# Projecting half of the queries with tokens on partitions, in plain float32, in a linear-attention and gated-MLP kernel

## The chip, the cores and the metric

The kernel runs on one core of a Trainium2 chip. The metric is the device time of one execution in microseconds (us), less is better. The engines named below are the profile's: PE is TensorE's matmul stream, PEld its weight loads, DVE is VectorE, ACT is ScalarE, POOL is GpSimd, and SP is SyncE, whose queue (SPq) issues every DMA of this kernel.

## The reference

Attention with a feature map, followed by a gated feed-forward layer with a convolution over tokens:

```python
# q, k, v: (8 batches, 8 heads, 576 tokens, 64); w_phi: (64, 128)
def phi(x):
    proj = np.einsum('bhsd,df->bhsf', x, w_phi)
    proj = proj - np.max(np.abs(proj), axis=-1, keepdims=True)
    return np.concatenate([np.exp(proj), np.exp(-proj)], axis=-1)
q_p, k_p = (phi(q), phi(k))
kv = np.einsum('bhsf,bhsd->bhfd', k_p, v)
z = np.sum(k_p, axis=2)
num = np.einsum('bhsf,bhfd->bhsd', q_p, kv)
den = np.einsum('bhsf,bhf->bhs', q_p, z)[..., None] + 1e-06
attn = num / den                       # heads joined: x is (8, 576, 512)

h = np.maximum(x @ w_in, 0.0)          # w_in (512, 1024)
conv_out = sum(conv_w[k] * h shifted by k - 1 tokens, for k in 0..2)
out = (h / (1 + np.exp(-conv_out))) @ w_out   # w_out (1024, 512)
```

## The kernel before, in words

**Tiling.** The 8 heads of a batch are taken as two units of four heads, numbered `qd` 0 and 1, so that there are 16 units. A unit holds two stacks, and a stack holds a pair of heads, 64 features of each, on the 128 partitions. Its tokens are cut into five groups: group 0 is one tile of 128 tokens (the last 64 tokens of both stacks), groups 1 to 4 are two tiles each (`n` is 1 or 2). So a unit has nine tiles of 128 tokens by two heads.

**Precision.** Where a number has to be kept to float32, most of the kernel splits it into a float32r high part and a float32r remainder and multiplies three times (high by high, high by low, low by high). In a few places it multiplies plain float32 numbers, which shows in the trace as two MATMUL records for one instruction.

**Queries.** A group of queries must end as feature-major values in PSUM (features on partitions, tokens along the row), less the largest absolute value of each token's projection, on which ACT takes two exponentials (L399). The kernel has two ways to get there.

- *Tokens on partitions* (the `lo is None` branch, batches 0 and 1, which is what `NQ_F32 = 4` units means). One DMA loads the group (L191). `project` multiplies each tile once by the float32 weights of both heads (L220); DVE takes the absolute maximum (L228) and subtracts it (L230) into an SBUF tile called `qs`; PE transposes the result, two transposes for a tile, against an identity (L353). The projection and the transposed values each take one PSUM tile of the ring `gq`, which has two.
- *Features on partitions* (batches 2 to 7). Two DMAs load the group twice, once to each half of the partitions (L196). ACT writes the float32r rounding of it (L199), and POOL replaces the lower half by the remainder (L200). Two matmuls with stationary weights write the whole group, 512 columns wide for two tiles (L360, L364). DVE takes the maximum over blocks of 32 features with a transpose (L368), ACT moves three of four blocks together (L371, three small instructions), DVE finishes the maximum (L375 to L379), one small DMA writes it into two rows of the operand (L380), and a third matmul subtracts it in PSUM (L386). One PSUM tile of `gq` holds the group throughout.

After that both ways are the same: exponentials, a split into high and low parts (L60, L65), and the products with `kv` (`nm`, L420 and L432), between whose matmuls the next unit's key products (`kv`, L275 and L279) are placed one by one. Then ACT moves numerators and denominators out (L454, L459), and `x_process` divides.

**The feed-forward part.** Half a batch of tokens (288) is one step: `h_part` is 96 matmuls (`hp`, L509), `conv_process` does convolution and gate on POOL, DVE and ACT, `o_part` is 96 matmuls (`op`, L572) whose results ACT moves out (L577) ahead of a DMA.

**What sets the order.** The program is emitted by a planner at the end of the function. Attention groups are generators in a window of 16, the feed-forward part is one more generator, and each yields estimated PE times (`pe(330 * n)` for a projection, `pe(220 * n)` for its transposes; `pe(230 * n)` and `pe(115 * n)` for the other way) and waits. The planner compares how much of `ATT_PE` and `MOE_PE` is left and steps one or the other. Steps of attention from batch 1 on are given a priority offset of 300 for the scheduler, which orders each engine's instructions; some are given high priority beside it (the features-on-partitions maximum, the third matmul, the exponentials). Each engine works its own queue in order.

The functions that the difference touches, with the profile's line numbers:

Of the kernel before, what the change touches and what calls it, by code (L numbers as in the profile page):

```python
# [15 lines left out]
B, H, S, D = 8, 8, 576, 64  # L16
# [3 lines left out]
NQ = 2  # L20
# [10 lines left out]
NQ_F32 = 4  # L31
# [4 lines left out]
def kernel(  # L36
# [20 lines left out]
    def split(src, hi, lo, eng_hi, eng_lo):  # L57

        if eng_hi is nc.scalar:
            nc.scalar.activation(out=hi, in_=src, func=AF.Copy)  # L60
        elif eng_hi is nc.gpsimd:
            nc.gpsimd.tensor_scalar(out=hi, in0=src, scalar1=1.0, scalar2=0.0, op0=ALU.mult, op1=ALU.add)  # L62
        else:
            nc.vector.tensor_copy(out=hi, in_=src)
        eng_lo.tensor_tensor(out=lo, in0=src, in1=hi.bitcast(F32), op=ALU.subtract)  # L65
# [118 lines left out]
    def group_columns(g):  # L184
        return (512, 1) if g == 0 else ((g - 1) * 256 + (P if g > 2 else 0), 2)

    def load_split(src, b, qd, g, kind):
        c0, n = group_columns(g)
        if kind == "q" and 2 * b + qd < NQ_F32:
            raw = sb.tile([P, n * P], F32, name=f"{kind}r{b}_{qd}_{g}", tag=kind + "r", bufs=2)  # L190
            nc.sync.dma_start(out=raw, in_=src[b, qd, :, c0 : c0 + n * P])  # L191
            return n, raw, None
        if kind == "q":
            raw = sb.tile([P, 2, n * P], F32, name=f"qr{b}_{qd}_{g}", tag="qr", bufs=2)
            for h in range(2):
                nc.sync.dma_start(out=raw[D * h : D * h + D, :, :],  # L196
                                  in_=src[b, qd, :, c0 : c0 + n * P].rearrange("(i d) s -> d i s", d=D))
            x = sb.tile([P, 2, n * P], F32R, name=f"qx{b}_{qd}_{g}", tag="qs", bufs=2)
            nc.scalar.activation(out=x, in_=raw, func=AF.Copy)  # L199
            nc.gpsimd.tensor_tensor(out=x[D:P], in0=raw[D:P], in1=x[D:P].bitcast(F32), op=ALU.subtract)  # L200
            return n, x, x
        raw = sb.tile([P, n * P], F32, name=f"{kind}r{b}_{qd}_{g}", tag=kind + "r", bufs=2)
        nc.sync.dma_start(out=raw, in_=src[b, qd, :, c0 : c0 + n * P])
        hi = sb.tile([P, n * P], F32R, name=f"{kind}xh{b}_{qd}_{g}", tag=kind + "xh", bufs=2)
        lo = sb.tile([P, n * P], F32R, name=f"{kind}xl{b}_{qd}_{g}", tag=kind + "xl", bufs=2)
        split(raw, hi, lo, nc.gpsimd, nc.gpsimd)
        return n, hi, lo
# [36 lines left out]
    def k_process(b, qd, g):  # L244
# [4 lines left out]

        yield until(back("kp", 2), back("kv", 4))  # L250
        n, hi, lo = load_split(kT, b, qd, g, "k")
        v0 = 16 if g == 0 else 4 * (g - 1)
        v = sb.tile([P, 4 * VW], F32, name=f"v{b}_{qd}_{g}", tag="v", bufs=3)
# [77 lines left out]
    def q_process(b, qd, g):  # L331
# [4 lines left out]

        yield until(back("qp", 2))
        n, hi, lo = load_split(qT, b, qd, g, "q")
        yield wait(3000)
        yield until(back("tp", 2))  # L340
# [266 lines left out]
        active.append([now[0], g, False, lead[0]])  # L607

    MOE_PE = 2 * B * (8 * 1480 + 4 * 2960)
    ATT_PE = B * (18 * 330 + 72 * 215 + 18 * 345 + 8 * 6 * 270 + 4 * 250) + NQ_F32 // NQ * 18 * 205  # L610
    TAIL = TAIL_US * 1000
    left = {"a": ATT_PE, "m": MOE_PE}
    start = {}
# [28 lines left out]
    while moe is not None or chains or active:  # L642
        while chains and sum(1 for p in active if p[2]) < WINDOW:
            b, x, g, kind = chains.pop(0)
# [82 lines left out]
```

## Time and profile before

| | |
|---|---|
| median of 3 runs | 827.03 us (826.72 to 830.36) |
| profiled execution, time | 827.25 us |
| profiled execution, span from first to last instruction | 825.5 us |
| PE busy / PEld busy | 775.8 us / 744.0 us |
| DVE / ACT / POOL busy | 649.4 us / 627.4 us / 316.1 us |
| instructions | 17295 |
| mean granted TensorE clock | 0.981 |
| moved by DMA | 56.44 MB |

Durations below come from the one profiled execution. A MATMUL's recorded duration holds its latency, and neighbours overlap; what one costs in a dense stream is the distance from its start to the start of the next. Every busy time is that of the engine alone, so the engines' times overlap.

### The profile page before, as it was taken

To read this page: it belongs to the slowest core of one execution; us is meant where nothing else is said; L and a number is where in the kernel's file an instruction comes from. 1 tells how busy PE (TensorE), PEld (TensorE's weight loads), DVE (VectorE), ACT (ScalarE), POOL (GpSimd) and SP (SyncE) were. 2 spreads that over 40 slices of the span, in tenths; PEclk is the share of its full clock that TensorE was granted. 3 is DMA by queue.
4 is the path that set the end of the run, shared out by engine and by line. 5 is a ranking of instruction groups with operands and counts; after the bars stand their busy time and mean duration, and the time that the engine had idled before them with its cause. 6 is when DMAs were issued, how large, how long until landed. Compare 5 with 4: busy or idle time off the path is not lost. (4 is left out here: it accounts for less than half of the span.)

```text
span 825.5 us, 17295 instructions
## 1 busy us (share of the span) xinstructions
PE 775.8 (94%) x5972; PEld 744.0 (90%) x5972; DVE 649.4 (79%) x1378; ACT 627.4 (76%) x1372; POOL 316.1 (38%) x395
## 2 busy tenths in 40 slices
PE   6988889899999999999999999999999899999997
PEld 5866789798989889999989999999999899999997
DVE  5898999796887968889788798788888587766451
ACT  4787886859898797988888888798988779744322
POOL 5765564262524424344243352525335232211120
PEclk9998989989999999999999999999999899999999
DMA  5544422212222122222222222222222111000001
GB/s 168 179 131 122 130 65 70 66 37 68 67 64 74 38 84 68 68 71 66 78 68 65 69 70 63 70 61 74 62 81 59 51 39 31 10 30 30 22 23 43
DMA packets 66814, 56.44 MB, mean 68 GB/s; under 512 B 17832, under 2 KB 64680, under 8 KB 66728
## 3 DMA queue, kind: packets, MB, share of 16 engines
q1 hardware_dynamic: 66728, 55.35, 23.3%
q8 instruction: 47, 0.77, 0.4%
q14 instruction: 39, 0.32, 0.1%
HBM read 45.21 MB, written 9.44 MB: 66 GB/s over the span
## 5 line engine op out<-in xcount | busy, mean ns | idle before, releaser
L279 PEld LDWEIGHTS kv<-v,ke 128*128 128x128 f32 x1024 | 156.5, 195 | 10.8 <-ACT ke L260 5.2
L279 PE MATMUL kv<-v,ke 128*128 128x65 f32 x1024 | 161.4, 256 | 4.3 <-ACT ke L260 4.2
L539 DVE SCALAR_TENSOR_TENSOR c<-h,cw,c 128x288 f32<-128x288 f32 (+1 forms) x256 | 144.7, 574 | 23.1 <-POOL c L534 21.1
L534 POOL TENSOR_SCALAR c<-h,cw 128x288 f32<-128x288 f32 x128 | 82.3, 645 | 207.2 <-ACT h L517 142.7
L572 PE MATMUL op<-gh,wout_hi 128*128 128x288 f32 x512 | 153.0, 299 | 5.9 <-ACT os L577 5.0
L509 PE MATMUL hp<-xh,win_hi 128*128 128x290 f32 x512 | 154.2, 302 | 4.2 <-ACT h L517 3.3
L572 PE MATMUL op<-gl,wout_hi 128*128 128x288 f32 x512 | 152.3, 298 | 0.9 <-DVE gl L65 0.9
L509 PE MATMUL hp<-xl,win_hi 128*128 128x290 f32 x512 | 153.1, 299 | 0.1
L509 PE MATMUL hp<-xh,win_lo 128*128 128x290 f32 x512 | 152.7, 298 | 0.0
L572 PE MATMUL op<-gh,wout_lo 128*128 128x288 f32 x512 | 152.0, 297 | 0.0
L200 POOL TENSOR_TENSOR qx<-qr,qx 64x512 fp32r<-64x512 f32 (+1 forms) x60 | 77.6, 1294 | 111.2 <-ACT qx L199 102.3
L65 DVE TENSOR_TENSOR ql<-qe,qh 128x512 fp32r<-128x512 f32 x112 | 90.0, 822 | 22.0 <-ACT qh L60 21.7
L509 PEld LDWEIGHTS hp<-xh,win_hi 128*128 128x128 f32 x512 | 97.6, 191 | 7.5 <-ACT h L517 5.4
L572 PEld LDWEIGHTS op<-gh,wout_hi 128*128 128x128 f32 x512 | 97.0, 190 | 7.5 <-ACT os L577 5.9
L572 PEld LDWEIGHTS op<-gl,wout_hi 128*128 128x128 f32 x512 | 97.1, 190 | 1.7 <-DVE gl L65 1.2
L509 PEld LDWEIGHTS hp<-xl,win_hi 128*128 128x128 f32 x512 | 97.9, 191 | 0.7 <-DVE xl L65 0.2
L509 PEld LDWEIGHTS hp<-xh,win_lo 128*128 128x128 f32 x512 | 97.7, 191 | 0.5
L572 PEld LDWEIGHTS op<-gh,wout_lo 128*128 128x128 f32 x512 | 97.2, 190 | 0.5
L62 POOL TENSOR_SCALAR kxh<-kr 128x256 fp32r<-128x256 f32 (+1 forms) x80 | 42.3, 529 | 130.8 <-issue 62.6
L517 ACT ACTIVATE h<-hp 128x290 f32<-128x290 f32 x128 | 50.8, 405 | 40.1 <-PE hp L509 39.6
L432 PE MATMUL nm<-ql,kvh 128*65 128x256 f32 x224 | 69.5, 310 | 0.2 <-DVE ql L65 0.2
L432 PE MATMUL nm<-qh,kvl 128*65 128x256 f32 x224 | 69.2, 309 | 0.0
(99 smaller groups left out, 1879.3 us busy)
## 6 DMA issues: line engine op xcount, KB each, us to landing
qr<-in_qT_dram SPq DMA_DIRECT2D x112, 128.0 KB
v<-in_vt_dram SPq DMA_DIRECT2D x80, 130.0 KB
out_dram<-os SPq DMA_DIRECT2D x64, 144.0 KB
kr<-in_kT_dram SPq DMA_DIRECT2D x64, 128.0 KB
w_r<-in_w_in_dram SPq DMA_DIRECT2D x8, 512.0 KB
w_r<-in_w_out_dram SPq DMA_DIRECT2D x8, 512.0 KB
rr<-rc SPq DMA_DIRECT2D x128, 2.2 KB
qr<-in_qT_dram SPq DMA_DIRECT2D x28, 64.0 KB
```

The costliest lines, as they stand in the source:

```text
L62: nc.gpsimd.tensor_scalar(out=hi, in0=src, scalar1=1.0, scalar2=0.0, op0=ALU.mult, op1=ALU.add)
L65: eng_lo.tensor_tensor(out=lo, in0=src, in1=hi.bitcast(F32), op=ALU.subtract)
L200: nc.gpsimd.tensor_tensor(out=x[D:P], in0=raw[D:P], in1=x[D:P].bitcast(F32), op=ALU.subtract)
L279: ins = nc.tensor.matmul(out=kp[i][:, s, p0 : p0 + VW], lhsT=lhsT, rhs=v[:, (2 * t + i) * VW : (2 * t + i + 1) * VW], start=False, stop=(g ...
L432: ins = after(ins, lambda: nc.tensor.matmul(out=ps[:, i, o : o + w], lhsT=w_, rhs=x_, start=(k == 0), stop=(k == 5)))
L509: nc.tensor.matmul(out=ps, lhsT=w_, rhs=x_, start=(k == 0), stop=(k == 11))
L517: nc.scalar.activation(out=h4[:, f % 4, :], in_=ps, func=AF.Relu)
L534: nc.gpsimd.tensor_scalar(out=cv, in0=hs[:, o : o + TC], scalar1=cw[:, f, 1:2], scalar2=0.0, op0=ALU.mult, op1=ALU.add)
L539: nc.vector.scalar_tensor_tensor(out=cv[:, lo:hi], in0=hs[:, o + j - 1 + lo : o + j - 1 + hi], scalar=cw[:, f, j : j + 1], in1=cv[:, lo:hi ...
L572: nc.tensor.matmul(out=ps, lhsT=w_, rhs=x_, start=(k == 0), stop=(k == 23))
```

## The change

From batch 2 on, the units with `qd == 0` (the first half of each batch's queries) are loaded, projected and transposed as in batches 0 and 1; the units with `qd == 1` stay with features on partitions. Six of the twelve later units move, that is, six groups of one tile and 24 groups of two. Exponentials, splits, products and everything behind them stay. The planner's total for attention gets half of the difference between the two ways for each moved batch.

```diff
+    def plain(b, qd):
+
+        return 2 * b + qd < NQ_F32 or qd == 0
+
     def load_split(src, b, qd, g, kind):
         c0, n = group_columns(g)
-        if kind == "q" and 2 * b + qd < NQ_F32:
+        if kind == "q" and plain(b, qd):
             raw = sb.tile([P, n * P], F32, name=f"{kind}r{b}_{qd}_{g}", tag=kind + "r", bufs=2)
             nc.sync.dma_start(out=raw, in_=src[b, qd, :, c0 : c0 + n * P])
             return n, raw, None
...
     MOE_PE = 2 * B * (8 * 1480 + 4 * 2960)
-    ATT_PE = B * (18 * 330 + 72 * 215 + 18 * 345 + 8 * 6 * 270 + 4 * 250) + NQ_F32 // NQ * 18 * 205
+    ATT_PE = B * (18 * 330 + 72 * 215 + 18 * 345 + 8 * 6 * 270 + 4 * 250) + (NQ_F32 // NQ + (B - NQ_F32 // NQ) / 2) * 18 * 205
```

## The prediction

> **What bounds the kernel now.** I read the page first (busy times and the slices of the clock), then the busy time by stretch, then the chain that ended last, then PE's waits inside the middle stretch, and at last PE's instructions in order of time, to price the two ways of projecting.
>
> ```profile
> PE 775.8 (94%) x5972; PEld 744.0 (90%) x5972; DVE 649.4 (79%) x1378; ACT 627.4 (76%) x1372; POOL 316.1 (38%) x395
> PEclk9998989989999999999999999999999899999999
> ```
>
> PE is the fullest engine, but a share over the whole span mixes stages. By stretch (start to end, length, then busy us with the number of instructions for PE, PEld, DVE, ACT and POOL, then the granted clock and DMA):
>
> ```profile
> 60.00:100.00 40.00, 34.06 (x218) 28.65 (x216) 35.88 (x72) 31.62 (x68) 23.46 (x23) 0.91 0.46 131
> 100.00:140.00 40.00, 36.21 (x269) 34.01 (x270) 39.87 (x76) 30.52 (x69) 21.17 (x24) 0.91 0.23 63
> 165.00:717.00 552.00, 531.19 (x4220) 515.78 (x4221) 451.99 (x1017) 463.95 (x1048) 212.60 (x259) 0.99 0.22 62
> 717.00:825.50 108.50, 103.88 (x771) 102.87 (x769) 55.12 (x94) 39.18 (x64) 13.80 (x25) 1.00 0.08 28
> ```
>
> From 165 to 717 us, where batches 2 to 7 run, PE is busy 531.19 of 552 us, so only 20.8 us are there to be won back, while ACT has 88 us free and DVE 100. From 717 us only feed-forward matmuls are left, and the chain that ended last is one row of them after another:
>
> ```profile
> 717.28 12.80 PE op L572 x96
> 730.08 13.11 PE hp L509 x96
> ```
>
> So PE's own work is the bound in both stretches: a microsecond of work added to PE is a microsecond at the end, unless it fills one of the 20.8 idle ones. PE's waits in the middle stretch are these (us, times, longest):
>
> ```profile
> PE op L572 <- ACT os L577: 5.0, 3, 4.2
> PE qp L386 <- DMA qx<-qmp: 3.4, 4, 1.4
> PE hp L509 <- ACT h L517: 3.3, 6, 1.5
> PE kp L223 <- ACT num L459: 3.1, 2, 2.6
> PE qp L360 <- POOL qx L200: 2.8, 3, 1.1
> PE kv L279 <- ACT ke L260: 2.1, 2, 1.6
> PE qp L360 <- ACT qe L399: 1.1, 1, 1.1
> ```
>
> The chain of a features-on-partitions query group accounts for 3.4 + 2.8 + 1.1 = 7.3 us of them; the other ACT rows for 5.0 + 3.3 + 3.1 + 2.1 = 13.5 us.
>
> **The change part by part: PE's work.** Both ways are in this trace, and both stand somewhere in a dense stream, so I take start-to-start distances. A group of two tiles in plain float32 (batch 1), and one with features on partitions (its three matmuls, here of neighbouring groups), and two matmuls of a one-tile group:
>
> ```profile
> 134.85 1.03 PE L220 MATMUL qp<-wbd_f,qr 128*128 128x256 f32 x4
> 135.71 0.60 PE L353 MATMUL tp<-idn,qs 128*128 128x128 f32 x4
> 136.15 0.28 PE L420 MATMUL nm<-qh,kvf 128*65 128x64 f32 x2
> ...
> 334.28 0.39 PE L360 MATMUL qp<-qx,wq_hi 128*128 128x512 f32 x1
> 334.51 0.40 PE L386 MATMUL qp<-qx,wq_m 128*128 128x512 f32 x1
> 334.75 0.40 PE L364 MATMUL qp<-qx,wq_lo 128*128 128x512 f32 x1
> 334.99 0.28 PE L223 MATMUL kp<-wbd_hi,kxh 128*128 128x256 f32 x1
> ...
> 341.13 0.28 PE L360 MATMUL qp<-qx,wq_hi 128*128 128x256 f32 x1
> 341.25 0.28 PE L364 MATMUL qp<-qx,wq_lo 128*128 128x256 f32 x1
> 341.37 0.30 PE L572 MATMUL op<-gh,wout_lo 128*128 128x288 f32 x1
> ```
>
> Plain: 135.71 - 134.85 = 0.86 us for the projection (four records for two instructions) and 136.15 - 135.71 = 0.44 us for four transposes, 1.30 us together; a one-tile group is half, 0.65. Features on partitions: 334.99 - 334.28 = 0.71 us; a one-tile group is 3 x 0.12 = 0.36. A unit has four groups of two and one of one, so it costs 4 x 1.30 + 0.65 = 5.85 us against 4 x 0.71 + 0.36 = 3.20 us. The six moved units add 6 x 2.65 = **15.9 us** to PE. The weight loads of both ways hide beside matmuls in these distances already.
>
> The Trainium skill's page "TensorE: Matmul & The Clock Gate", section "Back-to-back issue gap", gives columns / 2.4 + 2.5 ns for the gap between matmuls when warm, which is 56 ns for a transpose's 128 columns. By that, an estimate, four transposes would take 0.22 us, the six units 6 x 4.5 x 0.22 = 5.9 us less, and PE's extra work would be 10.0 us. The trace differs (0.44 us), and I go by the trace.
>
> **What the other engines lose and gain.** Over all 60 features-on-partitions groups, the instructions on the tile `qx` (columns PE, PEld, ACT, POOL) and on `qmt` (DVE, ACT) were busy:
>
> ```profile
> 0.00:825.50 825.50, 56.10 (x180) 30.53 (x180) 35.49 (x60) 77.62 (x60) 0.98 0.24 68
> ```
>
> ```profile
> 0.00:825.50 825.50, 62.34 (x180) 38.24 (x180) 0.98 0.24 68
> ```
>
> Half of the groups go. ACT loses (35.49 + 38.24) / 2 = 36.9 us and gains nothing. POOL loses 38.8 us. DVE loses 31 us of maximum work there, and gains the plain maximum and subtraction:
>
> ```profile
> L230 DVE TENSOR_TENSOR qs<-qp,qm 128x512 f32<-128x512 f32 x16 | 10.8, 678 | 0.0
> L228 DVE TENSOR_REDUCE qm<-qp 128x4 f32<-128x512 f32 x16 | 10.8, 678 | 0.4 <-PE qp L220 0.4
> ```
>
> 24 x 1.36 + 6 x 0.68 = 36.6 us. (Two small DVE instructions a group, L377 and L379, also go, so DVE comes out about level.) None of this is on the path by itself: DVE, ACT and POOL have slack in the middle stretch. If that cover went, 36.6 us of DVE work would be the price; level DVE work is why I cost it at nothing.
>
> What relief on ACT is worth must be bounded. At one end nothing; at the other all 13.5 us of PE's waits on ACT. ACT goes from 84% (463.95 of 552) to about 77% of the stretch, and 4.2 of the 13.5 us are a single wait, so I take a quarter, **-3.4 us**. Of the chain's own 7.3 us of waits I take the moved half, **-3.65 us**; the ends are 0 and -7.3.
>
> **What SP's queue loses.** For each moved group one load in place of two and no small DMA:
>
> ```profile
> L196 SPq DMA_DIRECT2D qr<-in_qT_dram x120: 598/645/1379, 135.9 to 680.4; - x120
> L380 SPq DMA_DIRECT2D qx<-qmp x60: 642/678/738, 155.3 to 702.2; - x60
> ```
>
> That is 0.645 + 0.678 = 1.3 us of issue a group, some 40 us over 30 groups. A load's buffer now comes free when PE has projected the group two back, and no longer when POOL has subtracted:
>
> ```profile
> SPq L196 <- POOL qx L200: 46.4, 35, 4.3
> SPq L191 <- PE qp L220: 2.3, 3, 1.4
> ```
>
> A load that waits holds back the key, value, denominator, reciprocal and output DMAs behind it. These rows say 1.3 us a wait before (46.4 / 35) and 0.8 after (2.3 / 3), so I count no new loss here, and no gain, since the PE waits above name loads nowhere; the ends are 0 and the 3.4 us of PE's waits on DMA, counted already.
>
> **New waits.** The plain way takes two PSUM tiles of `gq` where the other takes one, and PE waits for DVE between projection and transposes. While batch 1 went this way (90 to 160 us, ten groups), PE waited for:
>
> ```profile
> PE qp L220 <- ACT qe L399: 1.2, 1, 1.2
> PE tp L353 <- DVE qs L230: 1.0, 1, 1.0
> PE qp L220 <- PE kv L279: 0.4, 1, 0.4
> ```
>
> 2.6 us for ten groups, so 7.8 us for 30 at that rate; the other end is 0. In that stage DVE was busy 39.87 of 40 us (from 100 us) against 452 of 552 in the stretch where the moved units will run, so I take half, **+3.9 us**. Behind a waiting transpose stands every later matmul, feed-forward ones too, since PE works in order.
>
> **The sum.** 827.25 (the profiled execution; 1.75 us of it lie outside its span) + 15.9 - 3.65 - 3.4 + 3.9 = **840.0 us**. The execution stands 0.2 us above the median of the runs, which I leave in the rounding.
>
> **The rivals.**
>
> *Relief wins* (faster). PE's waits on ACT are the place. If all 13.5 us go, with the chain's 3.65, and with them the stretch at half clock that followed the 4.2 us wait,
>
> ```profile
> 642.00:648.80 6.80, 5.38 (x21) 5.28 (x22) 1.29 (x2) 3.67 (x10) 1.12 (x1) 0.50 0.20 63
> ```
>
> worth half of 6.8, the time is 827.25 + 15.9 - 13.5 - 3.65 - 3.4 = 822.6 us. It decides from the point where the relief passes 15.9 us; the difference can be measured from about 20.0. For it: ACT is the releaser in most PE waits. Against: all of PE's idle time there is 20.8 us, and ACT keeps 93% of its work in the stretch. Chance 0.06.
>
> *Relief just pays* (the same rows, about three quarters of them): 828 us, chance 0.09.
>
> *The ring and DVE bite*. The full 7.8 us of new waits, one more stretch at half clock after one of them (3.4 us), no relief: 827.25 + 15.9 + 7.8 + 3.4 = 854 us. For it: the rows of batch 1 above. Against: the density of DVE there. Chance 0.10.
>
> *The plain way cools PE*. In the two stretches of 40 us from 60 to 140 us, where units of the plain way run, the granted clock is 0.91; that is 2 x 40 x 0.09 = 7.2 us lost in about two units. At 3.6 us a unit, six moved units lose 21.6 us: 840 + 21.6 = 862 us. Against: PE was idle 5.9 of 40 us from 60 us on and 3.8 from 100, which can explain it without the transposes, and 0.44 us of transposes in the some 9 us that a group has (552 / 60) is little. Chance 0.03. The same page of the Trainium skill, section "Part 4: PE-mode transpose", says that a transpose does not count as PE being busy for the clock gate; by that rule this rival is the outcome. The trace cannot separate it from idle time, since both stand in the same stretches.
>
> **How the numbers follow.** The forecast case has 0.72 and gives 840 us; its own range is 831 to 850. Relief wins 0.06, relief just pays 0.09, the ring 0.10, cooling 0.03. Changes under 0.5% (4.1 us) can't be told from none here. Faster 0.06; same 0.09; slower 0.72 + 0.10 + 0.03 = 0.85. The range, 829 to 852 us, leaves out relief that wins, part of the even case, cooling and most of the ring: about 0.18.
>
> **What the changed profile would show.** L220 and L353 at 72 + 6 x 9 x 2 = 180 records each; L360, L364, L386 and the ACT and POOL work on `qx` at half; ACT some 37 us less busy, POOL 39 less, DVE within a few us. PE's distances for a moved group at 0.86 + 0.44 us. The last stretch unchanged at about 108 us, starting 12 or 13 us later. PE's waits on `qx` and `qmp` about halved, and a few us of waits at L220 and L353. Wrong it would be if PE's idle time from 165 us on fell well below 10 us, if the stretch showed several pieces at half clock, or if the scheduler's new order moved waits of other matmuls (L509, L572, L279) by more than the 3.4 us that I gave them.

## The result and the profile after

The changed kernel takes 838.42 us (median of 7 runs, 832.95 to 842.06) against 827.03 us before (7 runs, 825.63 to 830.36): a ratio of 1.012, 95% interval 1.0089 to 1.0151, so 11.4 us slower. The forecast was 840.0 us. The execution that was profiled took 832.95 us, the fastest of the seven, which has to be kept in mind below: its span is 5.6 us longer than that of before, half of what the medians say.

Page and busy time by stretch of the changed kernel (columns: start and end, length, busy us with the number of instructions for PE, PEld, DVE, ACT and POOL, granted clock, DMA share, GB/s); the last two stretches meet where its last rows of feed-forward matmuls begin (723 us):

```profile
PE 784.6 (94%) x6098; PEld 755.0 (91%) x6098; DVE 633.9 (76%) x1288; ACT 598.0 (72%) x1252; POOL 266.1 (32%) x365
PEclk9998999999999999999999999999999999999999
```

```profile
165.00:717.00 552.00, 535.33 (x4289) 521.89 (x4288) 428.94 (x913) 429.06 (x918) 162.65 (x227) 0.99 0.20 56
165.00:723.00 558.00, 541.33 (x4334) 527.89 (x4333) 433.12 (x922) 432.44 (x926) 164.37 (x230) 0.99 0.20 56
723.00:831.10 108.10, 103.96 (x771) 102.96 (x769) 55.24 (x94) 39.27 (x65) 13.88 (x25) 1.00 0.08 28
```

The chain that ended last:

```profile
723.36 12.80 PE op L576 x96
736.16 13.12 PE hp L513 x96
```

The last stretch is as long as before (108.1 against 108.5 us) and starts 6 us later, where the prediction had 12 or 13. Over the whole span ACT fell by 29.4 us and POOL by 50.0. Between 165 us and there PE is idle 16.7 us in place of 20.8, and yet that stretch is longer, because PE has more to do. PE's waits in it (from L187 on, lines are 4 higher than before):

```profile
PE kp L227 <- ACT num L463: 4.0, 3, 1.6
PE qp L224 <- ACT qe L403: 2.2, 1, 2.2
PE hp L513 <- ACT os L581: 2.2, 2, 1.5
PE op L576 <- ACT os L581: 1.5, 2, 1.1
PE qp L364 <- issue: 1.2, 1, 1.2
PE hp L513 <- ACT h L521: 1.0, 1, 1.0
PE nm L436 <- DVE ks L234: 1.0, 1, 1.0
PE qp L390 <- DMA qx<-qmp: 0.9, 1, 0.9
PE qp L364 <- POOL kxh L62: 0.7, 1, 0.7
```

The projection and transposes stand where the change put them (six units more, 72 records to 180):

```profile
L224 PE MATMUL qp<-wbd_f,qr 128*128 128x256 f32 x180 | 51.3, 397 | 11.0 <-ACT qh L403 4.3 <-DMA qr<-in_qT_dram 3.2 <-ACT qe L403 2.8
L357 PE MATMUL tp<-idn,qs 128*128 128x128 f32 x180 | 33.9, 274 | 1.8 <-DVE qs L234 1.5 <-ACT qh L403 0.2
```

Part of both spans ran at half clock. Inside the stretch from 165 us these are the pieces of before (two, of which 642.00:648.80 stands in the prediction) and of after:

```profile
164.10:170.90 6.80, 4.99 (x21) 4.98 (x22) 6.80 (x11) 6.36 (x15) 2.83 (x3) 0.50 0.13 38
```

```profile
164.70:168.10 3.40, 3.40 (x17) 3.39 (x16) 3.40 (x7) 1.93 (x5) 1.09 (x3) 0.50 0.26 77
707.40:710.80 3.40, 3.14 (x13) 3.13 (x14) 1.96 (x3) 3.31 (x8) 0.51 (x1) 0.50 0.14 46
```

In such a piece a matmul of the feed-forward part starts 0.241 us after the one ahead of it, here in before:

```profile
643.83 0.44 PE L572 MATMUL op<-gl,wout_hi 128*128 128x288 f32 x1
644.07 0.44 PE L572 MATMUL op<-gh,wout_lo 128*128 128x288 f32 x1
```

At full clock the distance is 0.134 us. So 1 - 0.134 / 0.241 = 0.44 of PE's busy time in these pieces is lost: from 165 us on 0.44 x (4.99 + 5.38) = 4.6 us before, and 0.44 x (3.10 + 3.14) = 2.8 us in the profiled execution after (the first 0.3 us of its first piece lie ahead of 165 us). PE's work at full clock grew by (541.33 - 2.8) - (531.19 - 4.6) = 11.9 us, idle time fell by 4.1 and lost clock by 1.8, which leaves the 6 us. This is not yet all of the added work: ten records of L224 that the change added stand ahead of 165 us. The table at the end of the experiments takes the whole span.

### The profile page after: what moved, and what is told of

It reads as the page before. It is cut to its first block, busy times and chain, and to the rows that moved or that the text cites. A ratio compares the mean times of both kernels' runs of the same rounds, so it can differ in the third digit from the quotient of the medians.

```text
span 831.1 us, 17133 instructions
## 1 busy us (share of the span) xinstructions
PE 784.6 (94%) x6098; PEld 755.0 (91%) x6098; DVE 633.9 (76%) x1288; ACT 598.0 (72%) x1252; POOL 266.1 (32%) x365
## 4 chain that ended last, share of the span: by engine, by line
PE 61%; DVE 15%; ACT 13%; DMA 5%; issue 4%; SPq 1%; POOL 1%; ACTq 0%; DVEq 0%; POOLq 0%
PE hp L513 18%; PE op L576 17%; PE kv L283 7%; PE nm L436 7%; DVE c L543 4%; PE qp L224 3%; DMA den<-dr 2%; PE kp L227 1%; ACT c L547 1%; PE tp L357 1%; ACT dr L458 1%; ACT num L463 1%; DVE xf L489 1%; DMA rr<-rc 1%; PE kp L228 1%
## 5 line engine op out<-in xcount | busy, mean ns | idle before, releaser
L543 DVE SCALAR_TENSOR_TENSOR c<-h,cw,c 128x287 f32<-128x287 f32 (+1 forms) x256 | 144.2, 573 | 31.7 <-POOL c L538 29.9
L283 PEld LDWEIGHTS kv<-v,ke 128*128 128x128 f32 x1024 | 154.3, 193 | 9.2 <-ACT ke L264 3.9
L538 POOL TENSOR_SCALAR c<-h,cw 128x288 f32<-128x288 f32 x128 | 78.2, 613 | 261.7 <-ACT h L521 171.2
L283 PE MATMUL kv<-v,ke 128*128 128x65 f32 x1024 | 159.6, 254 | 2.2 <-ACT ke L264 1.9
L65 DVE TENSOR_TENSOR ql<-qe,qh 128x512 fp32r<-128x512 f32 x112 | 81.1, 744 | 25.5 <-ACT qh L60 25.1
L60 ACT ACTIVATE qh<-qe 128x512 fp32r<-128x512 f32 x112 | 66.9, 627 | 0.9
```

Source lines behind the costliest of these rows:

```text
L283: ins = nc.tensor.matmul(out=kp[i][:, s, p0 : p0 + VW], lhsT=lhsT, rhs=v[:, (2 * t + i) * VW : (2 * t + i + 1) * VW], start=False, stop=(g ...
L538: nc.gpsimd.tensor_scalar(out=cv, in0=hs[:, o : o + TC], scalar1=cw[:, f, 1:2], scalar2=0.0, op0=ALU.mult, op1=ALU.add)
L543: nc.vector.scalar_tensor_tensor(out=cv[:, lo:hi], in0=hs[:, o + j - 1 + lo : o + j - 1 + hi], scalar=cw[:, f, j : j + 1], in1=cv[:, lo:hi ...
```

## The experiments

Every kernel ran beside the kernel before on the same chip; the ratio is to that. A busy row is that of the stretch from 165 to 717 us (columns as above), so that PE's idle time can be compared: 20.8 us before, 16.7 us after. A trace is of one execution, and where its time is far from the median of its kernel, the text says so.

**Work and relief, each alone.** Work: the kernel before with extra matmuls in the moved units' groups.

```diff
             nc.tensor.matmul(out=tpf, lhsT=wq_lo, rhs=xf, start=False, stop=False, skip_group_check=True)
+            if qd == 0:
+                for w_ in (w, w, w // 2):
+                    nc.tensor.matmul(out=tpf[:, 0:w_], lhsT=wq_m, rhs=xf[:, 0:w_], start=False, stop=False, skip_group_check=True)
...
-            yield pe(230 * n)
+            yield pe(230 * n + (205 * n if qd == 0 else 0))
...   (and the planner's total, as in the change)
```

> The kernel before, with three more matmuls in each group of queries of the six units that the change moved (512, 512 and 256 columns wide for two tiles, half of that for one), put behind the second projection matmul; the planner's figures are raised as in the change. They multiply by the weights of the third matmul, so they add a small error to those groups' projections. By the distances in the trace of before (0.24, 0.24 and 0.12 us) they add 24 x 0.59 + 6 x 0.30 = 15.9 us to PE, as the change does, and take nothing off any other engine. Theory 1 (PE's work is the cost, relief elsewhere gives a few us back): 841 to 844 us, 3 to 5 us above the changed kernel. Rival (added matmuls mostly fill PE's idle time, and what the changed kernel lost is new waits): 827 to 833 us.

Measured: 864.93 us, ratio 1.0456 (1.0431 to 1.048), 38 us slower. Neither theory.

```profile
165.00:717.00 552.00, 521.35 (x4009) 502.03 (x4010) 425.49 (x951) 436.30 (x981) 194.33 (x247) 0.97 0.21 61
```

```profile
PE qp L389 <- DMA qx<-qmp: 6.9, 6, 2.0
PE qp L360 <- POOL qx L200: 6.9, 5, 3.2
PE kp L223 <- ACT num L462: 6.8, 6, 2.6
```

PE is idle 30.7 us where it was idle 20.8, and the granted clock is 0.97 where it was 0.99. The extra matmuls stand ahead of the maximum, so they also lengthen that chain; this run does not isolate work.

Relief: PE's three matmuls as before, the other engines relieved. This kernel leaves out the queries themselves and their maximum, so it serves for timing alone.

```diff
+            if qd == 0:
+                x = win_hi[0][:, 0 : 2 * n * P].rearrange("p (i s) -> p i s", i=2)
+                return n, x, x
             x = sb.tile([P, 2, n * P], F32R, name=f"qx{b}_{qd}_{g}", tag="qs", bufs=2)
...
+            if qd == 0:
+                for a in range(2):
+                    nc.vector.tensor_reduce(out=mt[:, a, 0:c], in_=tpf.rearrange("p (c f) -> p c f", f=32), axis=AX,
+                                            op=ALU.max, apply_absolute_value=True, apply_transpose=True)
+            else:   # the chain of the maximum, as before
...
```

> The kernel before, with the other engines relieved as in the change and PE's work as it was: the six units' query groups keep their loads and three matmuls, but multiply a constant tile of weights in place of the queries (so no rounding on ACT, no remainder on POOL), leave out the maximum (ACT's three copies, the small DVE work, the small DMA), and put two reductions of the whole PSUM tile on DVE (2 x 0.70 us, about what the change has there). Theory 1 (relief gives back a few us: half of the 7.3 us chain, a quarter of 13.5 us on ACT): 819 to 823 us. Rival a (ACT relief gives back most of PE's waits): below 815 us. Rival b (relief gives nothing): 826 to 829 us.

Measured: 837.51 us, ratio 1.0122 (1.0095 to 1.0148). With less to do on ACT, POOL and SP and nothing more on PE, the kernel is 10.6 us *slower*. (The profiled execution, 833.37 us, is the fastest of six.)

```profile
165.00:717.00 552.00, 528.81 (x4169) 513.94 (x4169) 430.74 (x918) 431.18 (x920) 165.23 (x227) 0.98 0.21 60
```

```profile
PE qp L363 <- ACT qe L407: 6.0, 4, 1.5
PE op L580 <- ACT os L585: 5.4, 4, 1.9
PE qp L363 <- ACT qh L407: 3.2, 1, 3.2
```

Idle time is 23.2 us, and a new wait leads: the first projection matmul, which has no load or rounding to wait for any more, waits for ACT's exponentials to free its PSUM tile. All three theories fall. ACT is busy 431.18 us here, as little as in the changed kernel (429.06), and PE's idle time is no lower than before. So relief of ACT, in the order that this kernel has, gave nothing, and something else costs time here.

**The planner's total.** The changed kernel with the old `ATT_PE`.

```diff
-    ATT_PE = ... + (NQ_F32 // NQ + (B - NQ_F32 // NQ) / 2) * 18 * 205
+    ATT_PE = ... + NQ_F32 // NQ * 18 * 205
```

> The changed kernel with the planner's old total for attention. Theory 1 (the total only shifts the order a little): 836 to 841 us, as the changed kernel. Rival (the new total is a part of the loss, by the order that it makes): 832 us or less.

Measured: 837.2 us, ratio 1.012 (1.0098 to 1.0142). Every instruction stands at the same place of its queue as in the changed kernel, so this is the changed program once more (the scheduler's order does not follow the planner's total), and its time confirms the change's.

**All units moved.**

```diff
     def plain(b, qd):
-        return 2 * b + qd < NQ_F32 or qd == 0
+        return True
...
-    ATT_PE = ... + (NQ_F32 // NQ + (B - NQ_F32 // NQ) / 2) * 18 * 205
+    ATT_PE = ... + B * 18 * 205
```

> All units of queries with tokens on partitions: twelve moved units where the change has six. Theory 1 (PE's work, 2.65 us a unit, less a little relief): about twice the change's loss, 847 to 853 us, with no more than one or two stretches at half clock from 165 us on. Rival (the plain way cools PE, 3.6 us a unit): above 865 us with several such stretches. Rival (the two PSUM tiles of the ring bite once every group takes two): above 857 us, with the waits at the projection and the transposes over 10 us.

Measured: 831.02 us, ratio 1.0048 (1.0025 to 1.0071): 4 us slower than before, and faster than with half of the units moved. The theory that the change's loss doubles falls, and so do both rivals.

```profile
165.00:717.00 552.00, 550.17 (x4440) 540.40 (x4440) 417.97 (x830) 401.45 (x804) 124.71 (x199) 1.00 0.18 50
```

```profile
PE kp L227 <- issue: 0.6, 1, 0.6
PE kv L283 <- ACT ke L264: 0.5, 1, 0.5
PE op L576 <- ACT os L581: 0.3, 1, 0.3
PE qp L224 <- ACT qe L403: 0.2, 1, 0.2
```

PE is idle 1.8 us of 552, at a granted clock of 1.00. Nearly all waits are gone, those that had nothing to do with queries too (`op` waiting for ACT, `kv` for ACT). PE is busier than in any kernel above, and almost nothing else takes time. Between before and this kernel 19 us of idle time in this stretch were paid back; half way there, the change got back 4.1.

**Half of the units, in one block.**

```diff
-        return 2 * b + qd < NQ_F32 or qd == 0
+        return 2 * b + qd < NQ_F32 or b < 5
```

> Six units moved as in the change, but all of batches 2 to 4 in place of half of every batch: the two ways meet once and not at every unit; the planner's total is that of the change. The traces so far: PE's stalls from 170 to 715 us come to about 27 us before, 21 us in the changed kernel and next to nothing with all twelve units moved. Theory A (stalls go with the number of units that stay with features on partitions, wherever they stand): 835 to 840 us, as the changed kernel, with about half of the stalls of before in its second half. Theory B (the meeting of the two ways at each unit makes stalls, which cost the changed kernel its relief): 829 to 833 us, with almost no stall while batches 2 to 4 run.

Measured: 837.38 us, ratio 1.0134 (1.01 to 1.0169): as the change, so theory A's time. The profiled execution, 832.53 us, is again the fastest of its runs. Busy by stretch, first of this kernel, then of before:

```profile
165.00:400.00 235.00, 233.18 (x1891) 228.30 (x1891) 183.26 (x360) 172.30 (x351) 58.59 (x94) 0.99 0.20 57
400.00:715.00 315.00, 302.61 (x2395) 294.64 (x2394) 250.33 (x554) 259.31 (x571) 103.81 (x133) 0.99 0.20 56
```

```profile
165.00:400.00 235.00, 223.85 (x1775) 216.37 (x1776) 195.14 (x442) 197.37 (x445) 95.66 (x117) 0.99 0.23 65
400.00:715.00 315.00, 305.34 (x2432) 297.41 (x2431) 255.18 (x571) 265.33 (x601) 116.29 (x141) 0.99 0.21 60
```

While only moved units run (to 400 us; the last of their transposes stands at 425), PE is idle 1.8 us against 11.2. Where the others run, it is idle 12.4 us against 9.7 (8.6 and 10.0 in two further traces of the order of before, met below), one wait of 4.4 us on `ke` among them. In this trace stalls go with the units that keep features on partitions, and those units stall *more* than in the order of before.

**Work on PE away from the query chain.**

```diff
                 for w_, x_ in ((wa, xa), (wa, xb), (wb, xa)):
+                    if k == 0 and 2 <= n < 14:
+                        nc.tensor.matmul(out=ps, lhsT=w_, rhs=x_, start=True, stop=True)
                     nc.tensor.matmul(out=ps, lhsT=w_, rhs=x_, start=(k == 0), stop=(k == 11))
...
-                    yield pe(740)
+                    yield pe(740 + (123 if p == 1 and 2 <= n < 14 else 0))
...
-    MOE_PE = 2 * B * (8 * 1480 + 4 * 2960)
+    MOE_PE = 2 * B * (8 * 1480 + 4 * 2960) + 12 * 8 * 123
```

> The kernel before, with the first of each twelve feed-forward matmuls (L509) of the half batches 2 to 13 issued twice; the second overwrites the first, so nothing else changes. 96 matmuls of 0.135 us are 13.0 us of work on PE in the same stretch as the change's, away from the chain of the query groups. Theory (work on PE comes to the end one for one): 838 to 841 us. Rival (a part fills PE's idle time): 830 to 836 us. Rival (any lengthening makes more stalls and half clock stretches, as in the run with work added to the query chain): above 845 us.

Measured: 853.61 us, ratio 1.0338 (1.0308 to 1.0367): 27.6 us for 13 us of work. That is the second rival's time, by idle time and not by more half clock (the table below).

```profile
165.00:717.00 552.00, 522.73 (x4133) 504.27 (x4132) 432.44 (x980) 445.83 (x1000) 210.22 (x251) 0.99 0.21 61
```

```profile
PE qp L386 <- DMA qx<-qmp: 5.2, 10, 1.2
PE nm L432 <- ACT num L459: 4.6, 2, 2.5
PE qp L360 <- POOL qx L200: 4.4, 4, 1.9
```

Idle time rose to 29.3 us. Here the query chain was not touched at all, and it stalls more all the same (L386 5.2 us against 3.4, L360 on POOL 4.4 against 2.8). The scheduler had put the instructions in another order.

**Is it the order?** Three kernels keep or exchange the planner's figures.

```diff
# the kernel before, with the plain way's figures for the six units, and the new total
-            yield pe(230 * n)
-            yield wait(4000)
+            yield pe((330 if qd == 0 else 230) * n)
+            yield wait(1700 if qd == 0 else 4000)
...
-            yield pe(115 * n)
+            yield pe((220 if qd == 0 else 115) * n)
```

> The instructions of the kernel before, every query group projected as before, emitted in the order of the change: for the six units the planner is given the figures of the plain way (330 and 220 ns a tile, a wait of 1700) and the new total. Theory O (the order of before is one with few stalls, and most other orders cost the units with features on partitions some 10 us more): 833 to 840 us, with stalls on PE from 170 to 715 us near 35 us. Rival (the order matters little; what the runs with added work lost beyond their work came from the work): 825 to 829 us.

```diff
# the changed kernel, with the old way's figures for the moved units, and the old total
+            old = 2 * b + qd >= NQ_F32
-            yield pe(330 * n)
-            yield wait(1700)
+            yield pe((230 if old else 330) * n)
+            yield wait(4000 if old else 1700)
...
-            yield pe(220 * n)
+            yield pe((115 if old else 220) * n)
```

> The instructions of the changed kernel, emitted in the order of before: the six moved units are given the figures of the features-on-partitions way (230 and 115 ns, a wait of 4000), and the old total stands. Theory O: if the old order is a good one for these instructions too, 827 to 833 us; if its figures must fit the way, 836 to 842 us as the change. Rival (the change's loss is PE's work alone): 837 to 841 us.

```diff
-TAIL_US = 24
+TAIL_US = 30
```

> The kernel before with a neutral turn of the planner: TAIL_US 30 in place of 24, which paces attention against the feed-forward part a little otherwise. No instruction is added or taken away. Theory O: another order, slower by up to 10 us: 828 to 838 us. Rival (the order matters little): 825 to 829 us.

Measured: 826.63 us (ratio 0.9997, 0.9979 to 1.0015), 838.08 us (1.0134, 1.0105 to 1.0162) and 827.09 us (1.0013, 0.9994 to 1.0031). But these three are no test of the theory. Compared name by name on every engine, without the numbers of buffers, the first and the third have exactly the order of before, and the second exactly that of the changed kernel: the scheduler makes its order whatever the planner's figures are here. They are repeats of two programs, 827 and 838 us. So the theory was asked again with turns that do move the queues and still add or remove nothing.

```diff
-WINDOW = 16
+WINDOW = 14
```

> The kernel before with 14 attention groups in the planner's window in place of 16: no instruction is added or taken away, but many stand elsewhere in their engines' queues (1844 lines of difference on DVE; 579 with the change's planner figures, 45 with the other pace). Theory O, in its narrower form (the order of before has few stalls, and an order that differs as much as those of the runs with added or removed work has some 10 us more): 832 to 842 us. Rival (the order matters little, and the loss beyond the work comes from the work or its absence): 825 to 829 us.

```diff
-AHEAD = 300
+AHEAD = 200
```

> The kernel before with a priority offset of 200 for attention in place of 300: again only the order differs (1420 lines on DVE). Theory O in its narrower form: 830 to 842 us. Rival (the order matters little): 825 to 829 us.

Measured: 835.32 us (ratio 1.01, 1.006 to 1.0141) and 842.41 us (1.0208, 1.0177 to 1.0239). The same instructions in another order cost 9.5 and 16.6 us. (The counts in the expectations hold renamed buffers too. In the traces, by operation and tile without buffer numbers, 191 of the 1378 instructions in DVE's queue stand elsewhere for the window and 402 for the offset. They are 368 for the work in the feed-forward part and 479 for the work in the query chain.)

The window of 14, busy time and PE's waits:

```profile
165.00:717.00 552.00, 529.45 (x4151) 510.84 (x4152) 446.94 (x1002) 461.02 (x1036) 205.63 (x253) 0.98 0.22 62
```

```profile
PE qp L386 <- DMA qx<-qmp: 6.1, 8, 2.0
PE hp L509 <- ACT h L517: 3.4, 5, 1.5
```

The offset of 200:

```profile
165.00:717.00 552.00, 522.52 (x4080) 505.64 (x4081) 436.54 (x989) 450.62 (x1008) 209.45 (x252) 0.98 0.22 62
```

```profile
PE kp L223 <- ACT num L459: 7.4, 7, 2.6
PE nm L420 <- ACT num L459: 6.2, 2, 3.6
PE qp L386 <- DMA qx<-qmp: 5.5, 6, 1.5
```

PE is idle 22.6 and 29.5 us in the stretch. The third matmul waiting for the small DMA takes 6.1 and 5.5 us, against 3.4 before. With the offset the waits on ACT grow beside it; with the window they do not. Idle time is not all of the loss, though: 9.3 and 17.9 us between the profiled spans. The table below puts the rest in more time at half clock and in more busy time of PE for the same matmuls. So an order by itself can cost about 10 us and more. That is shown for the instructions of before, where nothing else differs; that the runs above lost what they lost beyond their work in this way is the likeliest reading, not shown separately.

**Keys' way for the queries.** With all units moved PE's work is the bound, so the cheaper projection of the keys (split on POOL, three float32r matmuls) was tried for batches 2 to 7; the features-on-partitions code is removed.

```diff
     def plain(b, qd):
-        return 2 * b + qd < NQ_F32 or qd == 0
+        return 2 * b + qd < NQ_F32
...
-        if kind == "q":
-            raw = sb.tile([P, 2, n * P], F32, name=f"qr{b}_{qd}_{g}", tag="qr", bufs=2)
...
-            return n, x, x
         raw = sb.tile([P, n * P], F32, name=f"{kind}r{b}_{qd}_{g}", tag=kind + "r", bufs=2)
...
         split(raw, hi, lo, nc.gpsimd, nc.gpsimd)
...
-        if lo is None:
+        if True:
...   (and the planner's total, as with all units moved)
```

> All queries with tokens on partitions, those of batches 2 to 7 as the keys are: POOL splits them into a float32r high part and a remainder, and PE multiplies three times (0.12 us each for 256 columns, 0.72 us for a group of two) in place of plain float32 (0.86 us). Against the kernel with all units in plain float32 (831.0 us) PE saves 12 x (4 x 0.14 + 0.07) = 7.6 us, and POOL gets about 12 x (4 x 1.43 + 0.99) = 80 us. Theory (with no features-on-partitions units left PE does not stall, and its work alone sets the time): 822 to 825 us, less than before. Rival (POOL's split becomes a wait for the projection): 829 us or more, with waits of the projection on POOL.

Measured: 826.44 us, ratio 0.9999 (0.9981 to 1.0017): level with before, 4.6 us less than all units in plain float32 and not the 7.6 us of the theory.

```profile
165.00:717.00 552.00, 545.98 (x4580) 543.88 (x4580) 427.09 (x839) 403.18 (x808) 201.51 (x311) 1.00 0.17 49
```

```profile
PE qp L197 <- ACT qe L336: 2.1, 3, 0.9
PE kp L197 <- DVE ks L204: 1.6, 2, 1.0
```

PE is idle 6.0 us in the stretch, 4.2 more than with all units in plain float32. Over the whole span PE's work fell by 7.4 us (the table below), nearly the theory's 7.6; 3.1 us came back as idle time. The rival's waits of the projection on POOL come to 0.9 us, so neither was quite right. No version was faster than the kernel before.

**Idle time, half clock and work of every trace.** The whole span of each profiled execution in three parts (us): PE idle, that is, span less busy time; lost to half clock, 0.444 of the time that PE was busy in pieces with a clock of 0.50; and the rest of its busy time, which is its work at full clock. PE's recorded durations hold latency, so short waits can hide in the last column.

| kernel | time of the profiled execution | PE idle | lost to half clock | work at full clock |
|---|---|---|---|---|
| before | 827.25 | 49.6 | 12.0 | 763.8 |
| order of before, planner's figures of the change | 826.71 | 46.7 | 12.1 | 766.2 |
| order of before, other pace | 829.16 | 53.9 | 11.0 | 762.4 |
| the change | 832.95 | 46.4 | 7.0 | 777.7 |
| order of the change, old total | 837.43 | 47.9 | 8.7 | 778.9 |
| order of the change, old figures | 836.03 | 46.2 | 9.8 | 778.2 |
| all units moved | 830.94 | 31.2 | 7.1 | 790.5 |
| half of the units in one block | 832.53 | 43.5 | 10.2 | 777.0 |
| work in the query chain | 866.42 | 60.2 | 20.3 | 784.1 |
| relief alone | 833.37 | 53.1 | 13.9 | 764.5 |
| work in the feed-forward part | 853.61 | 61.0 | 10.1 | 780.8 |
| window of 14 | 836.59 | 51.5 | 15.1 | 768.2 |
| offset of 200 | 845.14 | 57.1 | 18.6 | 767.6 |
| keys' way | 826.43 | 34.3 | 6.8 | 783.1 |

Three traces of one program differ by up to 7 us in idle time and 4 us in work, so a single trace does not settle a difference of that size. Means of three against three give the change: work 764.1 to 778.2, idle time 50.1 to 46.9, half clock 11.7 to 8.5. That is 14.1 us more, 3.2 less and 3.2 less, together 7.7.

## Why the prediction was right, and where it was not

**The time and the side** came out as said: 838.4 us against 840.0, inside the forecast case's own range.

**PE's work (+15.9 us)** was the right term and about the right size: 14.1 us by the means of three traces each, 2.35 us a unit and not 2.65. All twelve units moved give (790.5 - 764.1) / 12 = 2.2. The rule of the Trainium skill's page "TensorE: Matmul & The Clock Gate", section "Back-to-back issue gap", would have given 10.0, so the row of the trace was the better guide. Why the measured unit is still some tenths below the row stays open.

**The waits (-3.65 of the chain, -3.4 on ACT, +3.9 new).** Their sum was near: idle time fell by 4.1 us from 165 us on, and by 3.2 over the whole span in the means, where I had 3.15. Row by row the chain's waits went from 7.3 to 2.8 us (L364 and L390 above), those on ACT that are quoted from 13.5 to 8.7, and the new waits were one of 2.2 us at the projection and none at the transposes; small waits elsewhere took some 3 us back. But what I gave as their cause failed. I made relief a share of ACT's load, to be added to the rest. With relief alone, in that kernel's order, ACT was as free as in the change, and PE's idle time did not fall.

The runs showed two other terms. First, where the features-on-partitions way is gone entirely, nearly all of PE's waits go with it (20.8 to 1.8 us idle). The two kernels that show this also have less work on ACT and another order, so which of these does it is not separated. Second, a new order of the queues can cost the units that stay 9.5 and 16.6 us with nothing else changed. Half of what all twelve units gave back would be 9.5 us of idle time, and the change got 4.1; by this reading the new order took back about 5. I had named moved waits of other matmuls as a sign of being wrong, from 3.4 us on, and gave them no place in the sum.

**What the sum left out** is half clock. It fell by 3.2 us in the means, for which I had a term in the rivals alone. So the terms that I did name come to 14.1 - 3.2 = 10.9 us by the traces against my 12.75, and the six profiled executions differ by 7.7 us where the medians differ by 11.4. The profiled execution of the change was the fastest of its program: one at 837.43 us, with every instruction in the same place, has 1.8 us more of half clock, 1.5 more of idle time and 1.2 more of work. To be within 1.6 us of the median is therefore partly luck. How much of the change's own 11.4 us is order stays open: the block run shows the direction, but no run changes the changed kernel's order alone.

**Relief wins** (822.6 us) did not happen, but what I held against it, that all of PE's idle time is 20.8 us, was no argument: in the kernel with all units moved that time is indeed won back (though not shown to be ACT's doing). There it failed on the doubled work. By the rows ACT would keep 92% of its work in the stretch, and not the 93% that I wrote.

**The ring and DVE**: the two PSUM tiles cost one wait of 2.2 us in the change and 0.2 us with every unit moved. This rival is out.

**Cooling** is out too. With 288 records of transposes in place of 72, the stretch from 165 to 717 us ran at a clock of 1.00, against 0.99 before, where the rival had several stretches at half clock. The Trainium skill's page "TensorE: Matmul & The Clock Gate", section "Part 4: PE-mode transpose", says that transposes do not count as PE being busy; no run here shows a cost of that; in all of them the transposes stand among matmuls.

**The other engines.** DVE did not stay level but fell by 15.5 us (8.9 of them in `ql`, L65, which the change does not touch: 90.0 to 81.1 us). ACT fell by 29.4 us where I had 37, POOL by 50.0 where I had 39. None of them is the bound in these stretches, so DVE's work could be left at nothing.

## What to carry to other kernels

Where a scheduler orders in-order queues, an edit of a few instructions makes a new order, and that alone can be worth 1 or 2% (835.3 and 842.4 us against 825.8 here). Before a difference of that size is put down to the edit, run the old kernel with a neutral turn that moves the order as much, count how much it moved, and take more than one trace of each program. Price a way of computing not only by its busy time but by how many engines a group crosses before PE can go on: the way that crosses PE, DVE, ACT, DVE and a DMA made PE wait in every kernel that had it, and the one that crosses PE, DVE and PE left 2 to 6 us of idle time in the two kernels that had only it. That the crossings are the cause is the likeliest reading, not shown separately. Such a gain may need the last of the old units to go: half way there, little of it was to be seen.

## What the runs showed of the hardware that was not expected

In these traces, from 160 us on, the clock falls to half for 3.4 or 6.8 us at a wait of PE, and so charges for it a second time. PE had been busy for 0 to 58% of the 3.4 us ahead of such a piece. An example of before: PE waited 4.2 us for ACT until 643.4 us, and the clock was half from 642.0 to 648.8. The run with work in the query chain has a mean clock of 0.972 and that with an offset of 200 one of 0.973, the kernel before 0.981 and the one with all units moved 0.989, so waits cost more than the idle time in a table of waits says: with the offset 7.0 us more of idle time went with 6.9 us more lost to half clock, against the means of before. Half the clock cost less than twice the time here: 0.241 us in place of 0.134 from one matmul of 288 or 290 columns to the next, a factor of 1.8.
